# Query rows of an image scored in 3.5 tiles of 128, with the leftover rows gathered by DMAs from GpSimd

## The chip, the cores and the metric

The kernel runs on one core of one Trainium2 chip. The metric is the device time of one execution in microseconds. Three runs of the kernel before took 830.34 us in the median (828.73 to 830.89).

## What is computed

Four images, 12 heads, 448 rows, head size 64. The scores are mixed over the heads before the softmax and again after it; the result goes through an RMS norm and a gated MLP.

```
scores = scale * q @ k.T                          # (4, 12, 448, 448)
scores = einsum('bhij,hg->bgij', scores, w_pre)   # mix over heads, before
attn   = softmax(scores - max, axis=-1)           # sum + 1e-9 below
attn   = einsum('bhij,hg->bgij', attn, w_post)    # mix over heads, after
x      = (attn @ v) as (1792, 768)
xn     = x / rms(x) * rms_g
out    = (silu(xn @ w_gate) * (xn @ w_val)) @ w_out
```

## The kernel before

The attention is the first 347 us or so, the MLP the rest; the change is in the attention alone.

The rows of an image are cut into four chunks: three of 120 rows and one of 100, so that the score tiles hold 460 rows for 448. For each chunk n and each pair of heads hp, `qk_mm` (line 138) multiplies four times 64 query rows with the keys of one head (fp32, 64x64 weights, 448 columns) into two PSUM banks. `qk_evac` copies one bank to SBUF on VectorE (line 158, tile `st`) and one on ScalarE (line 160). A DMA then gathers from `st` (line 177) so that in the tile `r` the partitions are 12 heads of 5 rows. All 24 qk pairs of an image, six for each chunk, cost the same, whatever the chunk holds.

The loop `for t in range(T + 24)` in `part_a` has one step for each pair (n, p) of row groups, 92 in all: six in each of the first three chunks of an image and five in the last one, whose fifth step is half a step (one PSUM bank in place of two, for the last 10 rows). A step does:

- `premix` (line 186, PSUM tile `sp`): the mix over heads for 2 x 2 groups of 5 rows;
- `rowmax` on VectorE (line 193, `nm`), `expo` on ScalarE (line 200, `e`), both for two banks, then `norm`: line 207 (`t`) and 209 (`rp`) on VectorE, and line 212 (`wn`) on GpSimd, which scales the second mix by the reciprocal of the sums;
- `postmix` of the step before (line 227, tile `pm`), 28 small matmuls for a step, whose weights are `e` and whose input is `wn`; the half step issues the same 28, with two halves alike;
- one or two units of `av_mm` (line 271, tile `av`), the product with v of a pair of chunks finished earlier, 240 columns wide;
- the qk pair that `qk_at` sets for this step, for a chunk that is up to two chunks ahead. On TensorE its matmuls stand between those of premix: half of premix, half of qk, the other half of each;
- the copies of `pm` into `at_all` (line 240 on VectorE, 242 on ScalarE), and on GpSimd one operation of the sums of x (lines 294 to 309).

The order on every engine is the order in which the code issues it. `qk_at` holds one pair for each of the steps 0 to 84; the first eleven pairs are done ahead of the loop. All gathers in the loop go by the queue of SyncE; GpSimd issues none there.

Of the kernel before, what the change touches and what calls it, by code (L numbers as in the profile page):

```python
# [18 lines left out]
RH = 5  # L19
# [3 lines left out]
OFF = [0, 120, 240, 360]  # L23
# [26 lines left out]
def attention_moe(ctx: ExitStack, tc, q, k, v, wpre, wpost, mask, ident, wgv, wo, rms_g, out):  # L50
# [33 lines left out]
    wk_pre = cst.tile([128, 64], F32, name="wk_pre")  # L84
    wk = cst.tile([128, HR], F32, name="wk")

    msk = pro.tile([128, 2, RH], F32, name="msk", tag="ksm1")
    we = pro.tile([128, H], F32, name="we", tag="ksm2")
    wp = pro.tile([128, H], F32, name="wp", tag="ksm3")

    def load_consts():
        nc.sync.dma_start(msk.rearrange("p a r -> p (a r)"), mask)
        nc.sync.dma_start(we, wpre)
        nc.sync.dma_start(wp, wpost)

    def setup():
        nc.vector.tensor_scalar(we, we, D ** -0.5, None, ALU.mult)
        nc.vector.memset(wk_pre, 0.0)
        for i, (o, w) in enumerate(((wk_pre[:, :HR], we), (wk, wp))):
# [24 lines left out]
    held = []  # L124
# [7 lines left out]
    def qk_mm(n, hp):  # L132
# [7 lines left out]
        return [[lambda j=j, u=u: one(j, u) for u in range(2)] for j in range(2)]  # L140
# [8 lines left out]

    def qk_evac(n, hp, j):  # L150
        h, np_ = 2 * hp + j, PAIRS[n % NC]
        ps = qps[n, hp][j]
        if n == 0 and h < 1 or n == 1 and h < 2 * AHEAD:
            st = pro.tile([128, S], F32, name="st", tag="st", bufs=11)
        else:
            st = pq.tile([128, S], F32, name="st", tag="st", bufs=12)
        if j:
            nc.vector.tensor_copy(st, ps[:, :S])
        else:
            nc.scalar.activation(st, ps[:, :S], AF.Copy)  # L160
        for i, (lo, hi) in enumerate(((0, EARLY), (EARLY, 2 * np_)) if n == 0 else ((0, 2 * np_),)):
            w, at_ = RH * (hi - lo), 2 * RH * lo
            if h < H - 1:
                parts = [(h, 2 * RH, at_, 2 * w)]
            else:
                parts = [(h, RH, at_, w), (64, RH, at_ + w, w)]
            for row, k_, src, many in parts:
                dst = rt[n][row : row + (k_ - 1) * GAP + 1 : GAP, lo:hi]
                if i:
                    held.append((dst, st[src : src + many]))  # L170
                else:
                    turn = h if row < H else h + 1
                    if n:
                        eng = nc.gpsimd if n == 1 and 6 <= h < 2 * AHEAD else nc.sync
                    else:
                        eng = nc.sync if turn % 2 else nc.gpsimd if turn < 6 else nc.scalar
                    eng.dma_start(dst, st[src : src + many])

    def premix(n, p):
        ps = banks(ps_s, "sp", halves_of(n, p))  # L180
        sps[n, p] = ps

        def one(u, v_):
            sl = slice(64 * u, 64 * u + 64)
            o = ps[u][64 * v_ : 64 * v_ + 64, :S]
            nc.tensor.matmul(o, wk_pre[sl], rt[n][sl, 2 * p + v_], start=True, stop=True)  # L186

        return [[lambda u=u, v_=v_: one(u, v_) for v_ in range(2)] for u in range(len(ps))]
# [25 lines left out]
    def postmix(n, p):  # L214
        ps = banks(ps_m, "pm")
        e, w = et.pop((n, p)), wn.pop((n, p))
        for u in range(2):
            u_ = min(u, len(e) - 1)
            for c in range(JC):
                for m in range(2) if c < JC - 1 else (u,):  # L220
                    j = min(2 * c + m, S // JT - 1) * JT
                    for v_ in range(2):
                        sl = slice(64 * v_, 64 * v_ + HR)
                        at_ = u * (JC - 1) + c if c < JC - 1 else JB - 1
                        o = ps[v_][64 * m : 64 * m + JT, : JB * HR].rearrange("p (s a i) -> p s a i", s=2, a=JB)
                        w_ = w[sl, u_].rearrange("p (s i) -> p s i", s=2)
                        nc.tensor.matmul(o[:, :, at_], e[u_][sl, j : j + JT], w_, start=True, stop=True)  # L227
        pm[n, p] = ps

    def evac_a(n, p, v_):  # L230
# [4 lines left out]
        lo, hi = SLOTS[n]  # L235
        a = 2 * RH * p + RH * v_
        dst = at_all[:, lo : hi + 1 : hi - lo, :, a : a + RH]
        src = pm[n, p][v_][:, : JB * HR].rearrange("p (s x r) -> p s x r", s=2, r=RH)
        if v_:
            nc.vector.tensor_copy(dst, src)  # L240
        else:
            nc.scalar.activation(dst, src, AF.Copy)
# [5 lines left out]
    def width(k):  # L248
        return sum(4 * RH * PAIRS[n % NC] for n in BLOCKS[k])
# [23 lines left out]
    def av_copy(k, i):  # L273
        ns = BLOCKS[k]
        w, full = [2 * RH * PAIRS[n % NC] for n in ns], 2 * 2 * RH * PAIRS[ns[0] % NC]
        xt[k, i] = [p2[0].tile([128, 2, width(k)], F32, name=f"xt{k_}", tag=f"xt{k_}", bufs=3) for k_ in range(2)]
        for t, x in zip(xt[k, i], xps.pop((k, i))):
# [3 lines left out]
            else:  # L281
                nc.scalar.activation(t[:, :, :full], x[:, :, :full], AF.Copy)
                rest = x[:, :, full:].rearrange("p a (u i) -> p a u i", u=2)[:, :, :, : w[1]]
                nc.scalar.activation(t[:, :, full:].rearrange("p a (u i) -> p a u i", u=2), rest, AF.Copy)
# [100 lines left out]
    for i, a in enumerate([(n, hp) for n in range(1, NCHUNK) for hp in range(H // 2)][AHEAD:]):  # L385
        qk_at[i].append(a)
# [13 lines left out]
    for n in range(NCHUNK):  # L400
        b, c = divmod(n, NC)
        if n > 2:
            for i in range(2):
                job(6 * n - 16 + 3 * i, load_q, n, 3 * i, 3, nc.sync)
# [8 lines left out]
    for t, todo_ in enumerate(list(qk_at)):  # L413
        for n, hp in todo_:
            if n % NC == NC - 1 and n + 1 < NCHUNK:
                job(t + 1, load_k, n // NC + 1, hp)
# [22 lines left out]
    def part_a(extra):  # L439
# [30 lines left out]
        for t in range(T + 24):  # L470
# [46 lines left out]
            for a in qk_at[t][1:]:  # L517
                alone(qk_mm(*a))
                for j in range(2):
                    qk_evac(*a, j)  # L520
# [625 lines left out]
def layout(inputs):  # L1146
# [7 lines left out]
    qt = np.zeros((B, 2 * D, H // 2, SP_), np.float32)  # L1154
    qt[..., :S] = pairs(q)
    ql = np.zeros((B, 2 * D, NC, H // 2, 128), np.float32)
    for c, p in enumerate(PAIRS):
        u, r, t = np.meshgrid(np.arange(2), np.arange(RH), np.arange(2 * p), indexing="ij")
        i = np.minimum(OFF[c] + (u * 2 * p + t) * RH + r, SP_ - 1)
        ql[:, :, c, :, : 4 * RH * p] = qt[..., i.reshape(-1)]  # L1160
        if c == 0:
            i = np.concatenate([x.reshape(-1) for x in (i[..., :EARLY], i[..., EARLY:])])
            ql[0, :, c, :, : 4 * RH * p] = qt[0][..., i]
# [17 lines left out]
    mix = np.zeros((2, 64, H), np.float32)  # L1181
    row = np.zeros((2, 64, RH), np.float32)
    for u in range(2):
        for r in range(RH):
            at = GAP * r + (np.arange(H) + u) % H
            mix[u, at], row[u, at] = inputs["w_pre"], eye_r[r]
# [4 lines left out]
        "wpre": mix.reshape(128, H),  # L1191
        "wpost": halves(np.repeat(inputs["w_post"], RH, axis=0)),
        "mask": np.concatenate([row.reshape(128, RH), halves(np.tile(eye_r, (H, 1)))], axis=1),
# [23 lines left out]
```

## Time and profile before

| | us |
|---|---|
| median of three runs | 830.34 |
| the profiled execution | 833.58 |
| its span | 831.7 |
| TensorE busy | 799.6 (96%) |
| VectorE busy | 633.1 (76%) |
| ScalarE busy | 509.0 (61%) |
| GpSimd busy | 354.1 (43%) |

The profile is of one execution. Busy times are unions of instruction intervals. The ends of matmuls are modelled, so a TensorE shown as busy may be waiting inside a step. The granted clock of TensorE was full throughout (0.998 over the span). A step is told below by the time at which its first row maximum begins on VectorE.

### The profile page before, as it was taken

Reading aid. Unit: us, or ns where it says so; the run is one execution under the profiler, and the core shown is the slowest. Engines: PE = TensorE matmul, PEld = TensorE weight load, DVE = VectorE, ACT = ScalarE, POOL = GpSimd, SP = SyncE. Lnnn points to the kernel's source line nnn. Section 1 sums busy time; section 2 is a strip of 40 time slices with the busy share of each in tenths; the row PEclk is TensorE's granted clock in tenths of the full one; section 3 lists DMA queues with packets and bytes.
Section 4 is the critical chain, followed back from the end, with each engine's and each line's share of the span. In section 5 each row is a group of like instructions: output and inputs, shape, how many; then the busy total and the mean of one; then the engine's idle time right before and its main releaser. Section 6 shows DMA issues by size and latency. Waiting matters only on the chain.

```text
span 831.7 us, 27130 instructions
## 1 busy us (share of the span) xinstructions
PE 799.6 (96%) x10918; PEld 488.9 (59%) x10918; DVE 633.1 (76%) x1318; ACT 509.0 (61%) x1129; POOL 354.1 (43%) x467
## 2 busy tenths in 40 slices
PE   7899987999989999899999999999999999999998
PEld 2567766877767767655555555555555555555555
DVE  5777877797878877789589978997889776547562
ACT  3676767677767775774444554455445555969850
POOL 7212343353435435771533532525344358462310
PEclk9999999999999999999999999999999999999999
DMA  7778778667886665373446544753656345566641
GB/s 209 200 218 222 221 231 233 194 192 209 223 237 181 202 202 155 105 240 122 138 140 189 140 146 111 214 183 106 180 147 198 101 154 178 137 208 177 180 142 67
DMA packets 82383, 146.15 MB, mean 176 GB/s; under 512 B 10527, under 2 KB 73277, under 8 KB 82259
## 3 DMA queue, kind: packets, MB, share of 16 engines
q1 hardware_dynamic: 80462, 140.81, 56.5%
q0 software_dynamic: 832, 2.06, 1.0%
q8 instruction: 86, 1.41, 0.7%
q10 hardware_dynamic: 965, 1.56, 0.6%
q14 instruction: 38, 0.31, 0.1%
HBM read 72.83 MB, written 32.00 MB: 126 GB/s over the span
## 4 chain that ended last, share of the span: by engine, by line
PE 91%; issue 3%; DMA 3%; DVE 2%; ACT 1%; POOL 0%; ACTq 0%; SPq 0%; POOLq 0%; DVEq 0%
PE pm L227 9%; PE av L271 8%; PE qk L138 8%; PE sp L186 8%; PE pg L715 6%; PE pv L717 6%; PE pv L715 6%; PE pg L717 6%; PE pv L716 6%; PE pg L716 6%; PE po L717 6%; PE po L716 6%; PE po L715 6%; DMA r<-st 2%; DMA q<-in_q 1%
## 5 line engine op out<-in xcount | busy, mean ns | idle before, releaser
L200 ACT ACTIVATE e<-sp,nm 128x448 f32<-128x448 f32 x180 | 114.3, 638 | 90.8 <-DVE nm L193 88.7
L186 PE MATMUL sp<-r,wk_pre 64*64 64x448 f32 x720 | 163.9, 541 | 1.6 <-ACT e L200 1.0
L138 PE MATMUL qk<-k,q 64*64 64x448 f32 x768 | 153.6, 559 | 7.5 <-DMA q<-in_q 4.5
L193 DVE TENSOR_REDUCE nm<-sp 128x1 f32<-128x448 f32 x180 | 110.5, 620 | 42.1 <-PE sp L186 18.5
L212 POOL TENSOR_SCALAR wn<-wk,rp 128x60 f32<-128x60 f32 x180 | 60.8, 352 | 190.7 <-DVE rp L209 129.2
L227 PEld LDWEIGHTS pm<-wn,e 60*64 60x64 f32 x5152 | 110.3, 134 | 50.0 <-POOL wn L212 22.2
L227 PE MATMUL pm<-wn,e 60*64 60x60 f32 x5152 | 111.3, 220 | 15.2 <-issue 12.6
L763 POOL TENSOR_TENSOR sg<-sg,u 128x448 f32<-128x448 f32 x36 | 46.7, 1297 | 150.4 <-ACT sg L760 103.0
L271 PE MATMUL av<-at_all,v 64*64 64x240 f32 (+4 forms) x1728 | 95.9, 322 | 3.8 <-issue 3.7
L716 PE MATMUL pv<-x,wh 128*128 128x448 f16 x264 | 93.0, 352 | 0.0
L717 PE MATMUL pv<-x,wl 128*128 128x448 f16 x264 | 93.0, 352 | 0.0
L715 PE MATMUL pg<-x,wh 128*128 128x448 f16 x264 | 93.0, 352 | 0.0
L715 PE MATMUL pv<-x,wh 128*128 128x448 f16 x264 | 93.0, 352 | 0.0
L716 PE MATMUL pg<-x,wh 128*128 128x448 f16 x264 | 93.0, 352 | 0.0
L717 PE MATMUL pg<-x,wl 128*128 128x448 f16 x264 | 93.0, 352 | 0.0
L717 PE MATMUL po<-h,fac 128*128 128x448 f16 (+1 forms) x258 | 89.8, 348 | 0.0
L715 PE MATMUL po<-h,fac 128*128 128x448 f16 (+1 forms) x258 | 89.8, 348 | 0.0
L716 PE MATMUL po<-h,fac 128*128 128x448 f16 (+1 forms) x258 | 89.8, 348 | 0.0
L715 PEld LDWEIGHTS <-wh 128*128 128x128 f16 x528 | 51.7, 98 | 48.2 <-issue 0.2
L716 PEld LDWEIGHTS <-wh 128*128 128x128 f16 x528 | 51.7, 98 | 48.3 <-issue 0.3
L717 PEld LDWEIGHTS <-wl 128*128 128x128 f16 x528 | 51.7, 98 | 48.2
L271 PEld LDWEIGHTS av<-at_all,v 64*64 64x64 f32 x1728 | 71.3, 134 | 7.5 <-issue 6.8
(167 smaller groups left out, 1564.4 us busy)
## 6 DMA issues: line engine op xcount, KB each, us to landing
r<-st SPq DMA_DIRECT2D x117, 210.0 KB
hraw<-td SPq DMA_DIRECT2D x84, 224.0 KB
wraw<-in_wgv SPq DMA_DIRECT2D x20, 768.0 KB
td<-keep SPq DMA_DIRECT2D x48, 224.0 KB
wraw<-in_wo SPq DMA_DIRECT2D x12, 768.0 KB
r<-st SPq DMA_DIRECT2D x44, 175.0 KB
v<-in_v SPq DMA_DIRECT2D x24, 256.0 KB
k<-in_k SPq DMA_DIRECT2D x24, 224.0 KB
```

Of the source, the lines that this page charges most:

```text
L138: nc.tensor.matmul(ps[j][m, :S], qt[n][sl, hp, m], kt[n // NC, hp][sl], start=True, stop=True)
L186: nc.tensor.matmul(o, wk_pre[sl], rt[n][sl, 2 * p + v_], start=True, stop=True)
L193: nc.vector.tensor_reduce(t, ps[:, :S], AX.X, ALU.max, negate=True)
L200: nc.scalar.activation(e, ps[:, :S], AF.Exp, bias=nmx.pop((n, p, u)), accum_out=sm[n, p][:, u : u + 1])
L212: nc.gpsimd.tensor_scalar(wn[n, p][:, u], wk, r[:, u : u + 1], 1.0, ALU.mult, ALU.mult)
L227: nc.tensor.matmul(o[:, :, at_], e[u_][sl, j : j + JT], w_, start=True, stop=True)
L271: nc.tensor.matmul(x, vt[b, hp][sl, j, c_], a, start=(c_ == 0), stop=(c_ == JC - 1))
L715: nc.tensor.matmul(ps, a, xh[:, kk, at_], start=(kk == 0), stop=False)
L716: nc.tensor.matmul(ps, a, xl_[:, kk, at_], start=False, stop=False)
L717: nc.tensor.matmul(ps, a2, xh[:, kk, at_], start=False, stop=(kk == KT - 1))
L763: nc.gpsimd.tensor_tensor(h, sg, u, ALU.mult)
```

## The change

The first three chunks of an image now carry 8 more query rows each, from the end of the fourth, so that their qk tiles are full (128). The fourth chunk has 64 query rows and needs three qk steps in place of six: one step now takes four heads of 64 rows. The rows that don't fit into the groups of `r` go into a new tile `rest` (four slots), by small DMAs that GpSimd issues at the end of a step: two after each third qk pair of chunks 0 to 2, and four after the last one of chunk 3. Premix of the first and the last step of chunk 3 reads `rest` with weights of its own. An image has 450 rows in groups, the fourth chunk's last step stays a half one, and its postmix issues 14 matmuls. Chunks 2 and 3 are both 55 wide for the product with v (220 columns for the pair, 110 for the last chunks alone in place of 120). `st` becomes one tile with 12 slots.

```diff
-OFF = [0, 120, 240, 360]
+OFF = [0, 120, 240, 350]
+WIDE = [60, 60, 55, 50]
+TILES = [128, 128, 128, 64]
+SPLIT = 6
...
+        def two(j, i):
+            sl, u = slice(64 * j, 64 * j + 64), (i + j) % 2
+            nc.tensor.matmul(ps[i][64 * u : 64 * u + 64, :S], qt[n][sl, 2 * hp + i], kt[n // NC, 2 * hp + i][sl], start=True, stop=True)
+
+        f = one if n % NC < NC - 1 else two
+        return [[lambda j=j, u=u: f(j, u) for u in range(2)] for j in range(2)]
...
     def qk_evac(n, hp, j):
...
+        if n % NC == NC - 1:
+            for u in range(2):
+                gather(n, 2 * (2 * hp + j) + (u + j) % 2, st[64 * u : 64 * u + 64, at_], 0, SPLIT, False)
+            if hp == 2 and j:
+                for i in range(2):
+                    for u in range(2):
+                        later.append((rest[100 + 12 * u : 112 + 12 * u, slot(n - 3 + i)], st[64 * u + 60 + 2 * i : 64 * u + 62 + 2 * i, :6]))
         else:
...
+            if hp % 3 == 2 and j:
+                half = hp // 3
+                x = st[:, 6 * half : 6 * half + 6]
+                later.append((rest[30 * half : 30 * half + 30, slot(n)], x[120:125]))
+                later.append((rest[64 + 18 * half : 82 + 18 * half, slot(n)], x[125:]))
+
+    def rest_out():
+        for dst, src in later:
+            nc.gpsimd.dma_start(dst, src)
+        later.clear()
...
+        def rows(sl, i):
+            if not kind:
+                return rt[n][sl, i - 2 * last]
+            return rest[sl, slot(n - 3 + (i if p == 0 else 2))]
...
+        if len(e) == 1:
             for c in range(JC):
-                for m in range(2) if c < JC - 1 else (u,):
...
+                for m in range(2) if c < JC - 1 else (0,):
+                    for u in range(2):
+                        one(ps[u], u, u, c, m if c < JC - 1 else u, e[0], w[:, 0])
...
-        w = 2 * RH * PAIRS[ns[0] % NC]
+        w = WIDE[ns[0] % NC]
...
-    for i, a in enumerate([(n, hp) for n in range(1, NCHUNK) for hp in range(H // 2)][AHEAD:]):
-        qk_at[i].append(a)
+    starts, t_ = {}, -1
+    for n in range(1, NCHUNK):
+        for hp in range(H // 2 if n % NC < NC - 1 else H // 4):
+            if n == 1 and hp < AHEAD:
+                continue
+            t_ = max(t_ + (2 if n % NC == NC - 1 and hp == 2 else 1), first[n - 2] + 1 if n > 1 else 0)
+            starts.setdefault(n, t_)
+            qk_at[t_].append((n, hp))
...
         load_q(2, 3)
+        nc.gpsimd.memset(rest, 0.0)
+        rest_out()
         for hp in range(AHEAD):
             alone(qk_mm(1, hp))
             for j in range(2):
                 qk_evac(1, hp, j)
+        rest_out()
...
             if back(0) and t < T - 2:
                 norm(*back(0))
...
+            rest_out()
...
-    nc = bacc.Bacc("TRN2", target_bir_lowering=False, num_devices=1)
+    nc = bacc.Bacc("TRN2", target_bir_lowering=False, num_devices=1, dynamic_dma_scratch_size=8192)
```

What the table `qk_at` and the new DMAs do to the order is seen at three places. The first is TensorE in the second image, steps 33 to 35, before. `sp` is premix, `qk` the scores, `pm` the postmix of the step before, `av` the product with v; `k_0` to `k_5` are the keys of the six pairs of heads.

```order
L186 MATMUL sp<-r_123,wk_pre 64x448 x2
L138 MATMUL qk<-k_2_965,q_2207 64x448 x2
L186 MATMUL sp<-r_123,wk_pre 64x448 x2
L138 MATMUL qk<-k_2_965,q_2207 64x448 x2
L227 MATMUL pm<-wn,e 64x2x30 x28
L271 MATMUL av<-at_all,v_1_1173 64x240 x4
L271 MATMUL av<-at_all,v_1_1173 64x2x60 x4
L186 MATMUL sp<-r_123,wk_pre 64x448 x2
L138 MATMUL qk<-k_3_1036,q_2207 64x448 x2
L186 MATMUL sp<-r_123,wk_pre 64x448 x2
L138 MATMUL qk<-k_3_1036,q_2207 64x448 x2
L227 MATMUL pm<-wn,e 64x2x30 x28
```

The same place in the changed kernel:

```order
L226 MATMUL sp<-r_126,wk_pre 64x448 x4
L265 MATMUL pm<-wn,e 64x2x30 x28
L333 MATMUL av<-at_all,v_1_1124 64x220 x4
L333 MATMUL av<-at_all,v_1_1124 64x2x55 x4
L226 MATMUL sp<-r_126,wk_pre 64x448 x2
L149 MATMUL qk<-k_4_1012,q_2126 64x448
L149 MATMUL qk<-k_5_1014,q_2126 64x448
L226 MATMUL sp<-r_126,wk_pre 64x448 x2
L149 MATMUL qk<-k_4_1012,q_2126 64x448
L149 MATMUL qk<-k_5_1014,q_2126 64x448
L265 MATMUL pm<-wn,e 64x2x30 x28
```

Step 33 has no qk left and the product with v is narrower; step 34 has the third and last qk of chunk 7, with the keys of two pairs; step 35 has none again. Over the loop 73 steps have a qk pair in place of 85: it is gone from the steps 9, 11, 12, 33, 35, 56, 58, 79 and 81 to 84.

The second place is GpSimd at the steps 33 to 36, before. `wn` is the scaled second mix, `xt` and `sum` the sums of x.

```order
L212 TENSOR_SCALAR wn<-wk,rp 128x60 x2
L301 TENSOR_TENSOR xt_3029<-xt_3028 128x440
L212 TENSOR_SCALAR wn<-wk,rp 128x60 x2
L308 TENSOR_TENSOR xt_3029<-xt_3029 128x220
L212 TENSOR_SCALAR wn<-wk,rp 128x60 x2
```

And changed:

```order
L254 TENSOR_SCALAR wn<-wk,rp 128x60 x2
L364 TENSOR_TENSOR xt_2616<-xt_2615 128x420
L254 TENSOR_SCALAR wn<-wk,rp 128x60 x2
L210 DMA rest<-st 12x1x448 x4
L371 TENSOR_TENSOR xt_2616<-xt_2616 128x210
L254 TENSOR_SCALAR wn<-wk,rp 128x60 x2
```

Four DMA issues now stand between the `wn` of step 34 and that of step 35; after each third pair of a wide chunk two stand there.

The third place is TensorE at the half step of the first image, changed; before, every `pm` row there reads x28.

```order
L226 MATMUL sp<-rest,wk_pre 64x448
L145 MATMUL qk<-k_3_882,q_1208 64x448 x2
L226 MATMUL sp<-rest,wk_pre 64x448
L145 MATMUL qk<-k_3_882,q_1208 64x448 x2
L265 MATMUL pm<-wn,e 64x2x30 x28
L333 MATMUL av<-at_all,v_2_1282 64x240 x8
L226 MATMUL sp<-r_125,wk_pre 64x448 x2
L145 MATMUL qk<-k_4_1012,q_1208 64x448 x2
L226 MATMUL sp<-r_125,wk_pre 64x448 x2
L145 MATMUL qk<-k_4_1012,q_1208 64x448 x2
L265 MATMUL pm<-wn,e 64x2x30 x14
```

Premix of the half step reads `rest` on both halves of the partitions, and its postmix, one step later, has 14 matmuls.

## Rows read from the trace of the kernel before

**Rows 1.** The page: span, and busy time of each engine.

```profile
span 831.7 us, 27130 instructions
PE 799.6 (96%) x10918; PEld 488.9 (59%) x10918; DVE 633.1 (76%) x1318; ACT 509.0 (61%) x1129; POOL 354.1 (43%) x467
```

**Rows 2.** Windows: loop, five steps; us, then busy PE PEld DVE ACT POOL.

```profile
21.27:347.19 325.92, 303.74 (x7968) 230.32 (x7964) 254.47 (x673) 232.58 (x620) 133.37 (x293) 0.99 0.70 204
53.26:56.27 3.01, 3.01 (x74) 1.86 (x72) 2.41 (x7) 2.38 (x7) 0.60 (x2) 1.00 0.86 203
292.95:295.88 2.93, 2.93 (x92) 2.37 (x88) 2.52 (x6) 2.62 (x8) 1.00 (x3) 1.00 0.71 215
310.37:314.91 4.54, 3.87 (x108) 3.25 (x104) 3.03 (x10) 3.05 (x10) 1.41 (x5) 1.00 0.57 161
314.91:319.12 4.21, 4.03 (x109) 3.37 (x104) 2.62 (x6) 3.01 (x8) 2.61 (x5) 1.00 0.26 83
...
328.14:331.29 3.15, 3.15 (x108) 2.51 (x110) 2.40 (x10) 2.09 (x6) 1.87 (x8) 1.00 0.66 213
```

**Rows 3.** Timeline of one step, 292.7 to 295.9: start, length, engine, line.

```profile
292.73 0.60 POOL L212 TENSOR_SCALAR wn<-wk,rp 128x60 f32<-128x60 f32 x2 [1.38 <-DVE rp L209]
...
292.95 1.38 DVE L193 TENSOR_REDUCE nm<-sp 128x1 f32<-128x448 f32 x2 [0.39 <-PE qk L138]
...
293.10 1.19 PEld L227 LDWEIGHTS pm<-wn,e 60*64 60x64 f32 x54 [0.20 <-POOL wn L212]
...
294.27 0.83 PE L271 MATMUL av<-at_all,v 64*64 64x240 f32 x15
294.43 0.64 ACT L200 ACTIVATE e<-sp,nm 128x448 f32<-128x448 f32 x1
...
294.84 0.63 PE L186 MATMUL sp<-r,wk_pre 64*64 64x448 f32 x2
...
295.28 0.16 DVE L207 TENSOR_SCALAR t<-s 128x2 f32<-128x2 f32 x1
...
295.88 0.32 POOL L212 TENSOR_SCALAR wn<-wk,rp 128x60 f32<-128x60 f32 x1 [1.93 <-PE sp L186]
295.88 0.62 DVE L193 TENSOR_REDUCE nm<-sp 128x1 f32<-128x448 f32 x1 [0.17 <-PE sp L186]
```

**Rows 4.** Timeline, a step without qk: its two row maxima.

```profile
328.14 1.10 DVE L193 TENSOR_REDUCE nm<-sp 128x1 f32<-128x448 f32 x2
```

**Rows 5.** Groups by line, 21 to 347 us: busy, mean ns, idle before.

```profile
L186 PE MATMUL sp<-r,wk_pre 64*64 64x448 f32 x718 | 163.6, 541 | 1.5 <-ACT e L200 1.0 <-DMA r<-st 0.3
L138 PE MATMUL qk<-k,q 64*64 64x448 f32 x678 | 142.0, 547 | 1.7 <-issue 1.1 <-DMA q<-in_q 0.4 <-DVE t L207 0.2
...
L227 PE MATMUL pm<-wn,e 60*64 60x60 f32 x5064 | 109.7, 220 | 15.2 <-issue 12.6 <-DVE nm L193 1.1 <-POOL wn L212 0.7
...
L212 POOL TENSOR_SCALAR wn<-wk,rp 128x60 f32<-128x60 f32 x179 | 60.5, 352 | 190.0 <-DVE rp L209 128.5 <-PE sp L186 20.0 <-DVE square L602 7.6
...
L158 DVE COPY st<-qk 128x448 f32<-128x448 f32 x85 | 52.2, 614 | 0.0
...
L538 DVE TENSOR_SCALAR wac<-wac 128x384 f32<-128x384 f32 x8 | 2.7, 341 | 0.0
```

**Rows 6.** Timeline of GpSimd alone: the start, and two sums in the loop.

```profile
14.33 4.60 POOL L458 MEMSET r<- 128x5376 f32 x1
...
19.39 2.38 POOL L177 DMA_DIRECT2D r<-st  x4
23.93 0.61 POOL L212 TENSOR_SCALAR wn<-wk,rp 128x60 f32<-128x60 f32 x2 [2.15 <-DVE rp L209]
...
141.00 0.66 POOL L308 TENSOR_TENSOR xt<-xt 128x220 f32<-128x220 f32 x1
...
314.46 1.12 POOL L294 TENSOR_TENSOR xt<-xt,xt 128x440 f32<-128x440 f32 x1
```

**Rows 7.** The chain that ended last, 20 to 33 us: start, length, what.

```profile
26.84 3.55 DMA r<-st
```

More of the change, by code (lines that the diff above doesn't have):

```diff
@@ L148, in alone, with gather @@
         in_turn(*parts)
+    def gather(n, h, src, lo, hi, held_):
+        w, at_ = RH * (hi - lo), 2 * RH * lo
+        if h < H - 1:
+            parts = [(h, 2 * RH, at_, 2 * w)]
+        else:
+            parts = [(h, RH, at_, w), (64, RH, at_ + w, w)]
+        for row, k_, from_, many in parts:
+            dst = rt[n][row : row + (k_ - 1) * GAP + 1 : GAP, lo:hi]
+            x = src[from_ : from_ + many]
+            if held_:
+                held.append((dst, x))
+            else:
+                turn = h if row < H else h + 1
+                if n:
+                    eng = nc.gpsimd if n == 1 and 6 <= h < 2 * AHEAD else nc.sync
+                else:
+                    eng = nc.sync if turn % 2 else nc.gpsimd if turn < 6 else nc.scalar
+                eng.dma_start(dst, x)
@@ L161, in qk_evac @@
[L161 to L177, printed above, removed]
+        st = st_1 if n == 1 else st_all
@@ L181, in premix, with one @@
         sps[n, p] = ps
-        def one(u, v_):
+        last = n % NC == NC - 1
+        kind = int(last and p in (0, PAIRS[-1] - 1))
+        def rows(sl, i):
+            if not kind:
+                return rt[n][sl, i - 2 * last]
+            return rest[sl, slot(n - 3 + (i if p == 0 else 2))]
+        def one(u, v_, o):
             sl = slice(64 * u, 64 * u + 64)
-            o = ps[u][64 * v_ : 64 * v_ + 64, :S]
-            nc.tensor.matmul(o, wk_pre[sl], rt[n][sl, 2 * p + v_], start=True, stop=True)
-        return [[lambda u=u, v_=v_: one(u, v_) for v_ in range(2)] for u in range(len(ps))]
+            nc.tensor.matmul(o, wk_pre[sl, kind], rows(sl, 2 * p + v_), start=True, stop=True)
+        if len(ps) == 1:
+            return [[lambda u=u: one(u, 0, ps[0][64 * u : 64 * u + 64, :S])] for u in range(2)]
+        return [[lambda u=u, v_=v_: one(u, v_, ps[u][64 * v_ : 64 * v_ + 64, :S]) for v_ in range(2)] for u in range(2)]
     def rowmax(n, p):
@@ L1152, in pairs @@
         return x.reshape(B, H // 2, 2, S, D).transpose(0, 2, 4, 1, 3).reshape(B, 2 * D, H // 2, S)
[L1154 to L1163, printed above, removed]
+    qt = pairs(q)
+    ql = []
+    for b in range(B):
+        parts = []
+        for c in range(NC):
+            many = 2 * PAIRS[c] if c < NC - 1 else SPLIT
+            u, r, t = np.meshgrid(np.arange(2), np.arange(RH), np.arange(many), indexing="ij")
+            i = OFF[c] + WIDE[c] * u + RH * t + r
+            if c == 2:
+                i = np.where(t == 11, OFF[3] + WIDE[3] * u + 40 + r, i)
+            i = [i] if b or c else [i[..., :EARLY], i[..., EARLY:]]
+            i = [x.reshape(-1) for x in i]
+            at = np.arange(2 * RH)
+            if c < NC - 1:
+                more = [(30, 35, 45)[c] + (at // RH * WIDE[3] + at % RH)[:8]]
+            else:
+                more = [a + (at // RH * WIDE[3] + at % RH)[8:] for a in (30, 35)]
+            i = np.concatenate(i + [OFF[3] + x for x in more])
+            assert len(i) == TILES[c] and i.max() < S
+            parts.append(qt[b][..., i].reshape(2 * D, -1))
+        ql.append(np.concatenate(parts, axis=1))
+    ql = np.stack(ql)
     kl = pairs(k)
```

123 lines of the change are left out of this document (75 added, 48 removed).

## The prediction

> **What bounds the kernel now.** I read the head of the page first: TensorE is busy 96% of the span, the next engine 76% [rows 1]. That invites the reading that every microsecond taken off TensorE is a microsecond gained. The windows say where to doubt it. From the first step's row maximum to the 92nd's the loop takes 325.92 us [rows 2], 3.58 us a step, but an undisturbed step takes 2.93 us with qk and one unit of av, and 3.01 us with qk and no av at all [rows 2]. A whole unit of av (0.83 us, [rows 3]) costs such a step nothing, so TensorE's work is not what such a step lasts.
>
> So I followed one step through its timeline [rows 3]. The row maximum of step 77 starts at 292.95. The second exponential ends at 294.43 + 0.64 = 295.07, the sums are read at 295.28, and the scaled mix wn begins at 295.88: 2.93 us after the row maximum. The postmix of step 76 began to load at 293.10, 0.37 after its wn at 292.73. After it, postmix and av hold TensorE until premix of step 78 begins at 294.84, 1.74 later, and its row maximum starts 1.04 after that, at 295.88. These make a circle that closes every second step: postmix, av, premix, row maximum, exponential, sums, wn, postmix: 1.74 + 1.04 + 2.93 + 0.37 = 6.08 us for two steps, 3.04 for one, against 2.93 in this window. Neither the qk matmuls nor the copies of their result are links of that circle; qk only stands between the halves of premix and delays the second row maximum.
>
> Where a step has two units of av, TensorE does bind: steps 82 and 83 last 4.54 and 4.21 us with 3.87 and 4.03 of TensorE in them, and a step with two units and no qk lasts 3.15 [rows 2]. The rest of the average is single stalls, the first of them a gather that step 3 waits for from 26.84 on, 3.55 us [rows 7].
>
> **The change part by part.** All terms are against the profiled execution, 833.58 us, and carried over unchanged to the median of 830.34.
>
> Twelve steps lose their qk. *Steps 82 to 84* (two av): 4.54 and 4.21 become something like 3.15 with the same small stalls; I take the change in TensorE's busy time, 3.87 - 3.15 = 0.72 and 4.03 - 3.15 = 0.88, and 0.8 for the third: 2.4 gained. *Steps 9 and 12* (no av): VectorE's queue is the circle there, 2.41 busy of 3.01 [rows 2]; a copy of 0.614 [rows 5] goes out of it. I take 0.6 each: 1.2. Bounds for these: 0 and 0.8 each. *Steps 33, 56 and 79* (one av): two row maxima side by side take 1.10 [rows 4] where they take 1.38 around qk [rows 3], so the circle is 0.28 shorter. It could be nothing, since it helps only every second step's circle, or 0.61, a whole copy. I take 0.3, the row's: 0.9.
>
> *Steps 11, 35, 58 and 81* follow the four DMA issues on GpSimd. An issue in the start takes 2.38 / 4 = 0.595 us [rows 6], and the loop has none, so this is the one price without a row of its own place. From below, the issue is no cheaper than a wn of 0.352 [rows 5]; from above I allow twice the row, 1.2. At 0.595 four take 2.38. Wn of the step before starts about when this step's row maximum does (295.88 and 295.88, [rows 3]) and takes 0.6; then 2.38, then the sum at 0.66 [rows 6], so this step's wn starts 3.64 after the row maximum. Without qk it would be due 2.93 - 0.28 = 2.65 after it. It is late by 1.0, and against before by 0.7. Postmix is queued behind it on TensorE, and av and the next premix behind postmix. I charge 0.6 at 35, 58 and 81 (1.8 lost) and nothing at 11, where no sum stands between. Bounds: 0 (issue of 0.352) and 3.1 each (issue of 1.2).
>
> The pairs of issues: 21 fall in the loop. A pair, wn and the longest of the sums (1.12, [rows 6]) make 1.2 + 0.6 + 1.1 = 2.9 of a step of 2.93, so it just fits. GpSimd sits idle 190.0 us before the 179 wn, about 2.1 us for each step [rows 5]; that idle time is the cover. I charge 0.5 for all, between 0 and, at 1.2 for an issue, 21 x 0.6 = 12 less what the cover takes, some 6.
>
> [...]
>
> Narrower av: 36 units of the pairs of chunks 2 and 3 go from 240 to 220 columns. 0.83 x 20 / 240 = 0.07, less where half the matmuls are 120 wide: 0.06. A unit lies in every second circle, so half counts: 36 x 0.06 / 2 = 1.1; with 0.2 for the 110-wide units: 1.3 gained. Bounds 0 and 2.5.
>
> Postmix of the four half steps: 28 fewer records each at 109.7 / 5064 = 0.0217 us [rows 5], 0.6 of TensorE; half counts in the loop, all at the end: 1.0 gained together. Bounds 0 and 2.4.
>
> At the start GpSimd gets a memset of a third of one that took 4.60 (1.53), and six DMA issues at 0.595 ahead of the first wn: 5.1 us. It was through at 19.39 + 2.38 = 21.77, and wn started at 23.93 [rows 6], so this wn slips by 3.0. What follows it waits for the gather until 30.39 anyway [rows 7], so most is hidden; I charge 0.8, between 0 and 3. Copies into `st` wait for the new DMAs' reads of the slot; after chunks 7 and 11 the next write comes two steps later: 0.3 charged, up to 4.
>
> TensorE has 96 + 112 = 208 of its 7968 matmul records in the loop [rows 2] fewer, 2.6%. It stands 12.6 us before postmix waiting for nothing that the profile shows [rows 5]; in proportion that is 0.3, and with the same before other groups I take 0.4 gained. SyncE's queue keeps 52 gathers an image, the smaller ones in chunk 3. The MLP is untouched.
>
> Gained: 2.4 + 1.2 + 0.9 + 1.3 + 1.0 + 0.4 = 7.2. Lost: 1.8 + 0.5 + 0.8 + 0.3 = 3.4. Net 3.8: 833.6 becomes 829.8 in a profiled execution, and 830.3 becomes 826.5 in the median.
>
> **The rivals.**
>
> *TensorE binds after all.* Then all that it loses is gained: 96 qk records at 142.0 / 678 = 0.209 [rows 5] are 20.1, postmix 2.4, av 2.5: 25 us. For it speaks the 96% [rows 1] and that postmix and premix begin while others still run; against it the step without av. The three-microsecond circle would have to give way partly: at 60% it is 15 us, 815.
>
> *GpSimd becomes the bound, and the kernel is slower.* One mechanism: each DMA issue stands between two wn, and wn feeds postmix directly. It decides from an issue of about 0.75 us on, where a pair with its sum no longer fits into a step. At 0.9, a pair with wn and a sum between 0.66 and 1.12, say 0.85, takes 3.25 and costs 0.3 (21 of them 6.3); each of three fours makes wn late by 3.6 + 0.6 + 0.66 - 2.93 = 1.9 (5.7). That is 12.0 in place of 2.3: 9.7 more than in the sum, 836. For it: GpSimd's spans are rough, and wn has no slack. Against it: four issues in a row took 2.38.
>
> *Nothing comes of it.* The circle takes in what single steps gain, since the next step's circle was not shortened; only steps 82 to 84 and the end pay, 2.4 + 0.5, against 3.4 lost: 831, no change.
>
> **How the numbers follow.** The forecast has 0.50, TensorE as bound 0.20, no change 0.16, GpSimd 0.14. A measurement of this kernel tells 0.3% from no change, 2.5 us: faster means under 827.8. The forecast at 826.5, uncertain by 3, is faster in 0.70, the same in 0.26; the first rival always faster; the third faster in 0.25 and the same in 0.70; the second slower in 0.90. Together: faster 0.35 + 0.20 + 0.04 = 0.59, same 0.13 + 0.11 + 0.02 = 0.26, slower 0.15. The range goes from 813, past the first rival, to 835, almost at the second; its upper bound holds the issue costs up to 0.85 us.
>
> **What would show it.** In the profile after: qk in 672 records in place of 768 and busy about 20 us less; TensorE's busy time in the loop down by more than the loop itself; steps 82 to 84 near 3.2 us each; a step of one av without qk at 2.6 to 2.9; wn of steps 35, 58 and 81 waiting for nothing but GpSimd's own queue, with postmix idle before it; DMA issues near 0.6 us. I am wrong on the circle if single steps without qk get as short as 2.3 us, on GpSimd if issues in the loop take over 0.75 us, and on the start if the first wn comes more than 5 us after the 23.93 of before.

## The result and the profile after

The changed kernel takes 841.0 us (median of 8 runs, 834.2 to 866.2), the kernel before 831.0 beside it: a ratio of 1.0108, 95% interval 1.0062 to 1.0155. It is slower by 1.1%, not faster by 0.5%. Here and below a time is the median of all runs, while a ratio leaves out slow executions, those more than 1.5% above the fastest of their kernel, up to five of twelve. The profiled execution took 839.06 us, span 837.3. Of its engines, TensorE is busy as long as before, GpSimd 35 us longer [rows 1]:

```profile
span 837.3 us, 26834 instructions
PE 799.9 (96%) x10710; PEld 475.0 (57%) x10710; DVE 632.6 (76%) x1311; ACT 501.7 (60%) x1121; POOL 389.3 (46%) x532
```

The windows of the loop and of four of its steps (us, then busy PE, PEld, DVE, ACT and POOL, granted clock, DMA share, GB/s; their edges lie up to 0.06 us off the row maxima): the loop lasts 3.2 us longer than in [rows 2], although TensorE is busy 0.75 us less in it. Steps 9, 35 and 82 follow, and step 84:

```profile
22.12:351.31 329.19, 302.99 (x7792) 216.85 (x7788) 254.24 (x665) 225.32 (x611) 170.04 (x360) 0.99 0.70 195
59.29:61.93 2.64, 2.57 (x72) 1.37 (x72) 1.97 (x6) 2.24 (x6) 0.60 (x2) 1.00 0.67 211
147.45:150.10 2.65, 2.58 (x86) 1.97 (x88) 2.09 (x5) 2.45 (x10) 2.28 (x6) 1.00 0.65 167
315.75:320.47 4.72, 3.47 (x112) 2.85 (x114) 2.46 (x9) 2.52 (x8) 2.60 (x7) 1.00 0.41 114
323.46:329.11 5.65, 5.65 (x175) 4.86 (x176) 3.96 (x13) 2.30 (x7) 4.27 (x8) 1.00 0.04 14
```

The groups of the loop that answer to [rows 5]: qk is two groups now, 96 records fewer and 142.0 - 100.4 - 16.1 = 25.5 us less busy. The loads for postmix wait 44.6 us for wn (33.9 in one_row and 31.2 in no_rest, two experiments below), and the issues take 0.58 us each:

```profile
L265 PEld LDWEIGHTS pm<-wn,e 60*64 60x64 f32 x4980 | 102.8, 135 | 58.8 <-POOL wn L254 44.6 <-issue 10.3 <-DVE nm L235 0.5
L145 PE MATMUL qk<-k,q 64*64 64x448 f32 x486 | 100.4, 555 | 3.1 <-issue 2.6 <-DMA k<-in_k 0.5
L254 POOL TENSOR_SCALAR wn<-wk,rp 128x60 f32<-128x60 f32 x179 | 59.3, 344 | 151.1 <-DVE rp L251 99.2 <-PE sp L226 17.9 <-PE qk L145 7.5
L210 POOL DMA_DIRECT2D rest<-st x64 | 36.9, 580 | 5.2 <-issue 2.1 <-DMA rest<-st 1.5 <-ACT wac L820 0.4
L149 PE MATMUL qk<-k,q 64*64 64x448 f32 x96 | 16.1, 549 | 0.4 <-ACT st L191 0.4
```

GpSimd at the start (start, length, instruction, then the idle time before it): the first wn comes at 29.17, 5.2 us after the 23.93 of [rows 6].

```profile
20.43 1.61 POOL L530 MEMSET rest<- 128x1792 f32 x1
22.34 2.34 POOL L210 DMA_DIRECT2D rest<-st  x4 [0.30 <-POOL rest L530]
24.75 2.41 POOL L179 DMA_DIRECT2D r<-st  x4
27.16 0.56 POOL L210 DMA_DIRECT2D rest<-st  x1
28.48 0.56 POOL L210 DMA_DIRECT2D rest<-st  x1 [0.76 <-DMA rest<-st]
29.17 0.61 POOL L254 TENSOR_SCALAR wn<-wk,rp 128x60 f32<-128x60 f32 x2
```

The chain that ended last holds the transfers themselves (start, length, what): two leftover DMAs where [rows 7] has one gather, and in the loop a gather and a load of k behind each other, 14.9 us.

```profile
22.95 5.25 DMA rest<-st
28.48 6.40 DMA rest<-st
...
217.30 8.55 DMA r<-st
225.87 6.36 DMA k<-in_k
```

### The profile page after: what moved, and what is told of

Same layout as the page of the kernel before. It is cut to its first block, busy times and chain, and to the rows that moved or that the text cites. A ratio compares the mean times of both kernels' runs of the same rounds, so it can differ in the third digit from the quotient of the medians.

```text
span 837.3 us, 26834 instructions
## 1 busy us (share of the span) xinstructions
PE 799.9 (96%) x10710; PEld 475.0 (57%) x10710; DVE 632.6 (76%) x1311; ACT 501.7 (60%) x1121; POOL 389.3 (46%) x532
## 4 chain that ended last, share of the span: by engine, by line
PE 79%; DMA 7%; DVE 5%; issue 3%; POOL 3%; ACT 2%; SPq 1%; ACTq 0%; DVEq 0%; POOLq 0%
PE pm L265 7%; PE pg L785 6%; PE pv L786 6%; PE pg L787 6%; PE pv L785 6%; PE pg L786 6%; PE pv L787 6%; PE sp L226 6%; PE po L786 6%; PE po L785 6%; PE po L787 6%; PE av L333 6%; PE qk L145 5%; DMA r<-st 3%; DMA rest<-st 1%
## 5 line engine op out<-in xcount | busy, mean ns | idle before, releaser
L226 PE MATMUL sp<-r,wk_pre 64*64 64x448 f32 x672 | 149.9, 548 | 6.1 <-ACT e L242 3.0
L235 DVE TENSOR_REDUCE nm<-sp 128x1 f32<-128x448 f32 x180 | 108.8, 618 | 39.8 <-PE sp L226 27.5
L265 PEld LDWEIGHTS pm<-wn,e 60*64 60x64 f32 x5040 | 103.9, 135 | 59.2 <-POOL wn L254 45.0
L145 PE MATMUL qk<-k,q 64*64 64x448 f32 x576 | 113.0, 577 | 8.9 <-DMA q<-in_q 4.1
L333 PE MATMUL av<-at_all,v 64*64 64x240 f32 (+6 forms) x1728 | 91.7, 314 | 2.0 <-issue 1.9
L333 PEld LDWEIGHTS av<-at_all,v 64*64 64x64 f32 x1728 | 69.1, 133 | 4.7 <-issue 4.4
```

The source lines that it names most:

```text
L145: nc.tensor.matmul(ps[j][m, :S], qt[n][sl, hp, m], kt[n // NC, hp][sl], start=True, stop=True)
L226: nc.tensor.matmul(o, wk_pre[sl, kind], rows(sl, 2 * p + v_), start=True, stop=True)
L235: nc.vector.tensor_reduce(t, ps[:, :S], AX.X, ALU.max, negate=True)
L265: nc.tensor.matmul(o[:, :, at_], e_[sl, j : j + JT], w_[sl].rearrange("p (s i) -> p s i", s=2), start=True, stop=True)
L333: nc.tensor.matmul(x, vt[b, hp][sl, j, c_], a, start=(c_ == 0), stop=(c_ == JC - 1))
```

## The experiments

Ratios are against the kernel before on the same chip, five rounds each; "after" is the changed kernel at 1.0108 (1.0062 to 1.0155). Each edit is to it unless said. A difference between two ratios carries the intervals of both.

### What the 64 leftover DMAs cost, and whether GpSimd's issues are it

**no_rest**, the DMAs not issued:

```
-        for dst, src in later:
-            nc.gpsimd.dma_start(dst, src)
         later.clear()
```

> The changed kernel without the 64 DMAs into rest (the tile stays zero, so the leftover rows of every image are scored as zeros; all else is issued as in the changed kernel). Theory A, the DMAs on GpSimd cost all that is lost: the loop's start is no longer late (the changed kernel's row maximum of step 8 came 8.4 us late) and postmix no longer waits for a wn behind an issue; the time falls from 841 to 822 to 828 us, 3 to 9 below the kernel before. Theory B, the loss sits in the new layout itself (three qk steps with two pairs of heads, four gathers a step on SyncE, premix of rest): 835 to 841. Theory C, the start alone: the start's 8 us come back, the loop stays where it is: 832 to 834.

Measured: 824.4 us, 0.9897 (0.9857 to 0.9936). The rest of the change gains 1%, and the DMAs take away 2.1%.

**dmas_alone**, the kernel before with `st` as one tile, the tile `rest`, its memset and the same 64 DMAs, whose result nobody reads:

```
+        later.append((rest[30 * half : 30 * half + 30, slot(n)], x[120:125]))
+            rest_out()
```

> The kernel before with the tile rest, its memset and the same 64 DMAs added at the same places (nothing reads rest; st is one tile of 12 slots, the descriptor scratch 8192 as in the changed kernel). Theory A: 831 plus 12 to 18, so 843 to 849, more than the changed kernel, since nothing of the saving is there. Theory B: 831 to 835. Theory C: 838 to 840, with the first wn at 29 us and the loop of the kernel before behind it.

Measured: 856.0 us, 1.0275 (1.0242 to 1.0309), more than any theory gave: in the old schedule the same DMAs cost 2.7%. In its trace no copy and no matmul waits for them, only GpSimd's own issues (0.9 us).

**rest_sp**, SyncE issues them:

```
-            nc.gpsimd.dma_start(dst, src)
+            nc.sync.dma_start(dst, src)
```

> The changed kernel with the 64 DMAs issued by SyncE in place of GpSimd. Theory A: GpSimd is free, the first wn is at 25.5 us and postmix waits for wn as before: 829 to 835. If it is the landing of these DMAs, not their issue, that costs (copies into st wait for the slot to be read), the time stays at 838 to 842, as SyncE's queue was over 0.8 busy and lands them later still. Theory B: 841 or more.

Measured: 860.9 us, 1.0360 (1.0319 to 1.0402). With GpSimd free of them it is worse. They stand in SyncE's queue behind the gathers and hold the slots of `st`: copies into it wait 31.9 us on ScalarE and 27.5 on VectorE.

**start**, the memset of `rest` directly behind that of `r1`, chunk 1's DMAs left to step 0:

```
         nc.gpsimd.memset(r_all[1], 0.0)
+        nc.gpsimd.memset(rest, 0.0)
```

> The changed kernel with the start alone changed: the memset of rest directly behind that of the second r tile (GpSimd stood idle there until 7.2 us), and the rest DMAs of chunk 1 left to the first step of the loop, behind its wn. Theory A: the first wn comes at 24 to 25 us in place of 29.2, and 4 to 7 us come back: 834 to 837. Theory C, the start alone makes the loss: 831 to 834. If the late start was hidden behind the gather that step 3 waits for, as I predicted: 839 to 842.

Measured: 840.2 us, 1.0057 (1.0021 to 1.0093). At most a part of the loss.

**one_row**, the same issues, but one row each:

```
-        later.append((rest[30 * half : 30 * half + 30, slot(n)], x[120:125]))
+        later.append((rest[30 * half : 30 * half + 1, slot(n)], x[120:121, 5]))
```

> The changed kernel with its 64 leftover DMAs still issued by GpSimd at the same places, but each moving a single row of one head (1 x 448) in place of 12, 18 or 30 rows; so the rest tile gets only a 12th to a 30th of its rows. It keeps the issues and takes away the load and nearly all of the landing time. Known: the changed kernel 841.0 us, without the DMAs 824.4, before 831 to 833. Theory 1 (the 64 issues of 0.55 to 0.62 us stand ahead of the wn products in GpSimd's queue, and TensorE waits for wn): 838 to 842, nothing regained. Theory 2 (the copies into st wait until the slot's leftover DMAs, which land 3 to 9 us after the issue, have read it): 827 to 835. Theory 3 (the 3072 added packets hold up SyncE's gathers): 825 to 829.

Measured: 826.7 us, 0.9926 (0.9894 to 0.9958). The 64 issues cost 0.3% over no_rest, give or take 0.5%, of the 2.1%. So the wn that waits behind them is not the loss, and "issues ahead of wn" falls.

**other_src**, all rows, but read from the input k:

```
-        x = st[:, 6 * half : 6 * half + 6]
+        x = k[0]
```

> The changed kernel with the same 64 DMAs of the same shapes into the same rows of rest, but read from rows of the input k in DRAM, which nobody writes, in place of st; so the leftover scores are not the right ones. Issues and traffic stay, the copies into st wait for no leftover DMA any more, and the issue waits for no copy. Theory 1 (issues ahead of wn): 838 to 842. Theory 2 (st held until the DMAs have read it): 826 to 832. Theory 3 (packets): 838 to 842.

Measured: 832.2 us, 0.9988 (0.9948 to 1.0029). Against one_row the bytes cost about 0.6%, give or take 0.5%; the last 1.2% goes when `st` isn't read. The packets change with it (3584 and 1792 bytes in place of 5376). What is dear, the hold on the slots, the reading or the packets, was open.

### The hold on the slots

**alt**, the halves of `st` in strict turn, so that a half is written again three steps after its DMAs:

```
+        turn = n // NC % 2 if n > 1 else 0
+        my = (at_ + 6 * turn) % H
```

> The changed kernel with the two halves of st taken in strict turn: the short chunk uses one half and the chunk after it begins with the other, so that a half is written again three heads' pairs (some 8 to 9 us) after its leftover DMAs were issued, in place of one step (2.6 us) at the ends of the images. Nothing else changes. Theory 1 (issues ahead of wn): 839 to 841, nothing. Theory 2 (st held): the waits for the slot in steps 36, 59 and 82 (sums 2.74, 1.82 and 1.16 us late there) go, 832 to 836. Theory 3 (packets): 839 to 841.

**spread**, at most one or two issues a step (at three image ends the last ones then read slots that the next chunk has already written):

```
-            rest_out()
+            rest_out(2 if len(later) > 2 else 1)
```

> The changed kernel with at most one leftover DMA issued in a step, or two where more than two are waiting, in place of two or four behind each other; the same 64 DMAs, some of them one to three steps later. Theory 1 (issues ahead of wn): the late wn of steps 35, 58 and 81 (1.15 to 1.70 us after t in place of 0.44) and those beside sum operations shrink, 830 to 836. Theory 2 (st held): the DMAs start later and the slots come free later, 840 to 846. Theory 3 (packets): 838 to 841.

**rows**, the slots interleaved, to cut the packets:

```
+        my = at_ % 6 * 2 + at_ // 6
```

> The changed kernel with the twelve slots of st interleaved: heads 0 to 5 of a chunk take the even slots, heads 6 to 11 the odd ones. Nothing else changes, but the six rows that a leftover DMA reads in one partition no longer lie behind each other, so it can't put three of them into one packet of 5376 bytes. Known: in the changed kernel 368 such packets between 45 and 350 us took 705 ns each, where three packets of 1792 bytes at 93 ns take 279; read from DRAM the same rows went in packets of 3584 and 1792 bytes at 198 and 107 ns, and the kernel took 832.2 in place of 841.0. Theory 2a (slots held, and held long because the long packets from 2 to 5 partitions are slow): packets of 1792 bytes, landing near 4.5 us in place of 5.8, 829 to 835. Theory 2b (slots held, and reading from so few partitions is slow however the packets are cut): 838 to 842. Theory 3 (the load alone): 839 to 841.

Measured: alt 838.8 us, 1.0057 (1.0018 to 1.0097); spread 851.4, 1.0230 (1.0176 to 1.0284); rows 841.4, 1.0116 (1.0082 to 1.0150). Spread shows that a hold can cost: VectorE's copies wait 17.2 us for leftover DMAs there. Alt takes the waits of copies away and gains half a percent, and its interval overlaps that of after. The edit of rows missed its aim: the packets were still of 5376 bytes, at 639 ns in the mean, so it tells nothing of their cutting; it stands as a second measurement of after.

**many_parts**, as many rows, each from a partition of its own, from the slot that is written again last; **wide_hold**, the same from the slot that is written again first; **few_free**, the old partitions, but the last slot read six times:

```
-  x[120:125]
+  x[:30, 5]                                   (many_parts)
+  x[:30, 0]                                   (wide_hold)
+  x[120:125, 5:6].to_broadcast([5, 6, S])     (few_free)
```

> The changed kernel with the same 64 DMAs of 12, 18 and 30 rows into the same places of rest, but each read from one slot of st, a row from each of as many partitions, in place of six slots of 2 to 5 partitions; so the leftover scores are not the right ones. The bytes stay, the packets can't be longer than 1792 bytes, one slot in six is held and that one the last to be written again. Theory 2a and 2b (slots held until slow transfers have read them): 826 to 833, packets near 95 ns. Theory 3 (the load alone): 836 to 841.

> As the run with one row from each of 12, 18 or 30 partitions (833.2, ratio 0.9983; packets of 3584 and 1792 bytes at 256 and 93 ns), but read from the first slot of each half (0, or 6) in place of the last: the slot that the next chunk writes first, so it is held as in the changed kernel. The leftover scores are not the right ones. Theory H (the hold of a slot until its leftover DMAs have landed makes the 1.2% between that run and the changed kernel): 838 to 842, with copies into st waiting for leftover DMAs. Theory P (the slow packets of 5376 bytes from 2 to 5 partitions make it, through the other transfers on the same 16 engines): 831 to 835, as packets stay short.

> The changed kernel with the same 64 DMAs from the same 2, 3 or 5 partitions, but the last slot of the half read six times in place of six slots; so the leftover scores are not the right ones. The slot that is held is the last that the next chunk writes. Theory H (hold): 831 to 835, no copy into st waits for them. Theory P (slow packets from few partitions): packets of 5376 bytes at 550 to 700 ns as in the changed kernel, 836 to 842.

Measured: many_parts 833.2 us, 0.9983 (0.9945 to 1.0021); wide_hold 831.1, 0.9964 (0.9926 to 1.0002); few_free 838.8, 1.0081 (1.0045 to 1.0118). In many_parts the packets were of 3584 and 1792 bytes (257 and 93 ns in the mean), longer than expected. In few_free no copy waits for a leftover DMA, and it loses 0.8%, nearly all: the slow reading needs no hold. The trace of wide_hold, of an execution of 843.3 us, shows no waiting copy either, since its DMAs land in 4.6 us (median) in place of 5.8; so it is a hold that never made anyone wait. Theory P stands. Theory H falls by few_free, and by far_few below, where copies do wait.

### Why the reading is slow

**far_few** and **step_four**, the same shapes from partitions far apart, and from partitions four apart:

```
-  x[120:125]      x[125:]
+  x[0:125:31]     x[10:103:46]    (far_few)
+  x[0:17:4]       x[84:93:4]      (step_four)
```

> The changed kernel with the same 64 DMAs in number and shape (2, 3 or 5 partitions by six slots of st), but the partitions far apart: 0, 31, 62, 93 and 124; 10, 56 and 102; 0 and 96 or 16 and 112, in place of 120 to 124, 125 to 127 and two neighbours; so the leftover scores are not the right ones. The slots are held as in the changed kernel. Theory P1 (slow because neighbouring partitions are read at once): packets of 5376 bytes near 3 x 93 = 280 to 400 ns, 831 to 836. Theory P2 (slow because few partitions are read, wherever they lie): 600 to 720 ns, 838 to 842.

> The changed kernel with the same 64 DMAs in number and shape, read from partitions four apart: 0, 4, 8, 12 and 16; 84, 88 and 92; two that are four apart for the short chunk. So the leftover scores are not the right ones. Known: from neighbours packets took 705 ns (1.0108), from partitions 31 to 96 apart 385 ns (1.0014). Theory D (what counts is the distance): four apart lies near neighbours, 550 to 700 ns, 836 to 842. [...]

Measured: far_few 835.9 us, 1.0014 (0.9983 to 1.0045); step_four 835.2, 1.0008 (0.9974 to 1.0043). The packets of 5376 bytes took 386 and 367 ns in the mean in place of 705. Four apart is as good as far, so theory D, the distance, falls. These two are the clean comparison with after and few_free: the packets are the same in number and size.

GpSimd's DMA queue between 45 and 350 us shows it: packets, MB, and the share that its packets took of the time of 16 engines. After:

```profile
q0 software_dynamic: 2595, 2.00, 5.7%
```

one_row:

```profile
q0 software_dynamic: 1728, 0.10, 0.4%
```

many_parts:

```profile
q0 software_dynamic: 1728, 1.98, 3.0%
```

few_free:

```profile
q0 software_dynamic: 2592, 2.00, 5.6%
```

far_few:

```profile
q0 software_dynamic: 2592, 2.00, 3.3%
```

step_four:

```profile
q0 software_dynamic: 2592, 2.00, 3.2%
```

The same 2 MB take 5.6 to 5.7% from neighbours and 3.0 to 3.3% from elsewhere, and the kernels fall into the same two groups, 1.008 to 1.012 and 0.996 to 1.001. The number of packets does not sort them: few_free, far_few and step_four have the same. The groups are less clean than these numbers: start and the versions that read the neighbours with other changes besides (alt above, three more below) have slow packets too and lie between, at 1.004 to 1.006.

The gathers on SyncE's queue are late with the slow packets. SyncE issues about 177 gathers in this stretch. Of them 8 to 13 took more than 1 us in no_rest, one_row, many_parts, far_few and step_four; in after it was 23, in few_free 21, their sum 154.3 and 153.8 us in place of 138.9 to 143.8. At the start the last eight gathers of chunk 0 and the six of chunk 1 take SyncE 20.2 us after and 20.3 in few_free, 18.5 in step_four, 16.8 in far_few and 14.6 in no_rest. After:

```profile
17.39 6.82 SPq L526 DMA_DIRECT2D r<-st  x8
24.32 13.34 SPq L179 DMA_DIRECT2D r<-st  x6
```

no_rest:

```profile
17.99 7.03 SPq L524 DMA_DIRECT2D r<-st  x8
25.14 7.56 SPq L179 DMA_DIRECT2D r<-st  x6
```

The traces also show where in the execution this counts. The row maximum of step 8 in after, few_free, far_few and step_four:

```profile
55.53 0.60 DVE L235 TENSOR_REDUCE nm<-sp 128x1 f32<-128x448 f32 x1
55.72 0.60 DVE L235 TENSOR_REDUCE nm<-sp 128x1 f32<-128x448 f32 x1
51.10 0.60 DVE L235 TENSOR_REDUCE nm<-sp 128x1 f32<-128x448 f32 x1
50.32 0.60 DVE L235 TENSOR_REDUCE nm<-sp 128x1 f32<-128x448 f32 x1
```

And from there to the row maximum of the last step, in the same order (window, us, then busy times as above):

```profile
55.53:351.25 295.72, 277.34 (x7272) 202.02 (x7276) 234.46 (x618) 207.25 (x565) 156.56 (x330) 1.00 0.70 197
55.72:351.93 296.21, 275.94 (x7272) 205.37 (x7276) 232.38 (x619) 207.57 (x565) 156.41 (x330) 0.99 0.69 197
51.10:348.50 297.40, 276.52 (x7272) 201.52 (x7276) 233.05 (x619) 207.40 (x565) 156.55 (x330) 1.00 0.67 197
50.32:349.73 299.41, 277.53 (x7272) 203.20 (x7276) 233.33 (x618) 207.58 (x565) 156.56 (x330) 1.00 0.67 196
```

Reading neighbours makes step 8 late by 4.4 to 5.4 us. Behind step 8 it makes nothing longer that these traces show, although there, too, 22 gathers in after take over 1 us on SyncE, and 10 and 13 in far_few and step_four. What does differ behind step 8 are the kernels without packets of 5376 bytes: 287.1 us in one_row, 290.0 in many_parts, 290.7 in other_src and no_rest, where those that have them take 291.9 (rows_alt_early, below) to 299.6 (alt); left aside are spread, whose copies wait, and wide_hold, whose traced execution took 843.3 us against a median of 831.1. Whether their shorter or fewer packets do that, no run separates. Each of these is one execution, and executions of one kernel lie several us apart; so this places the loss and does not size it.

That waits of copies are not the price is seen once more in far_few. Who waited for `rest` there (us, times), and how long its DMAs took to land:

```profile
L210 POOL DMA_DIRECT2D rest<-st x64: 547/566/622, 22.1 to 312.3; - x64
...
  DVE st L189: 6.6, 3
  ACT st L191: 4.3, 2
...
DMA to landing us min/median/max: 2.6/4.5/8.9
```

And after:

```profile
L210 POOL DMA_DIRECT2D rest<-st x64: 547/568/622, 22.3 to 315.0; - x64
...
  DVE st L189: 5.7, 3
  ACT st L191: 3.3, 3
...
DMA to landing us min/median/max: 3.0/5.8/8.8
```

The copies wait longer in far_few, which is the faster; what differs is the landing.

Why the packets are slow from neighbouring partitions (705 ns) and not from partitions four apart (367 ns), no run shows.

### Versions that keep the result

**alt_early**, alt with chunk 0's DMAs ahead of the load of q and the memset of `r2`; **rows_alt_early**, that with the slots interleaved; **one_each**, alt_early with one issue a step; **one_each_act**, that from ScalarE's queue:

```
+        rest_out()
         load_q(2, 0)
         nc.gpsimd.memset(r_all[2], 0.0)
```

```
+            rest_out(1 if t else 4)                                 (one_each)
+                (nc.gpsimd if many == 4 else nc.scalar).dma_start   (one_each_act)
```

> The halves of st in strict turn, as in the run of that alone (838.8, ratio 1.0057), and the start put in another order on GpSimd: the memset of rest directly behind that of r1, the four leftover DMAs of chunk 0 ahead of the load of q and the memset of r2 (so some 6 to 8 us earlier), those of chunk 1 left to step 0. All in the same packets. At the start the copies of chunk 2 into st wait for these four DMAs to land. Theory 2 (slots held): most of the 8.4 us that row max of step 8 was late at (55.5 in place of 47.1) goes, 829 to 834. Theory 1 (issues ahead of wn) or 3 (load): 837 to 840, as the issues and the bytes stay.

> All three together: slots of st interleaved, halves in strict turn, chunk 0's leftover DMAs early. Without any leftover DMA it was 824.4. Theory 2a: 824 to 830, faster than the kernel before (831) by 0.2 to 0.8%. Theory 2b: 828 to 834. Theory 3: 834 to 840.

> The version with the halves of st in turn and the early start (834.2, ratio 1.0056), with one leftover DMA issued in a step in place of two or four; with the halves in turn each still reads its slots before they are written again. Theory H: 832 to 836, nothing left to win, or the later ones hold a little more. Theory P: fewer slow packets at a time, 828 to 833.

> The same with ScalarE's queue issuing the leftover DMAs of steps 1 and later (one in a step); GpSimd keeps the eight of the start. When SyncE issued them the packets were of 1792 bytes at the usual 93 ns. An issue on ScalarE took 0.78 us at the start, and ScalarE idles some 0.6 to 1.9 us a step before its exponentials: 56 issues of 0.78 us are 44 us, of which 0 to 20 show. Theory P: packets short, 824 to 829 and the part of the issues that shows, so 826 to 838. Theory H: 834 and that part, 834 to 846.

Measured: alt_early 834.2 us, 1.0056 (1.0022 to 1.0090); rows_alt_early 835.8, 1.0039 (1.0010 to 1.0068); one_each 837.6, 1.0039 (1.0003 to 1.0076); one_each_act 916.9, 1.1033 (1.0983 to 1.1082). The first three gain 0.5 to 0.7% on after, with intervals that overlap its own, and none beats the kernel before: the slow packets are all still there (in alt_early at 717 ns, GpSimd's queue at 5.9% of the time of 16 engines). ScalarE's queue is far worse than either theory said, though an issue took 0.74 us where 0.78 was expected. Its packets were of 1792 bytes, at 173 ns in the mean:

```profile
L213 ACTq DMA_DIRECT2D rest<-st x56: 630/744/822, 35.4 to 402.2; - x56
```

56 of these are 42 us and the loss is 84, so more than the issues is late; what, stays open.

A version with its leftover rows in partitions four or more apart, and its right result, was not tried. By step_four (1.0008) and far_few (1.0014) that alone would come level with the kernel before and not beat it. It would cost, too, as the author reads the code, though no run shows it: with rows taken out between, the other 120 rows of a chunk no longer lie behind each other, and each of SyncE's gathers would have to be split.

## Why the prediction was wrong

- **The gains were right in sum, in part by luck.** 7.2 us were forecast; no_rest shows 1.03% of 830.3, 8.6 us (5.3 to 11.9). But the terms that can be followed step by step, from the trace before to that of no_rest, came out smaller than charged: steps 9 and 12 gave 0.8 of 1.2, steps 33, 56 and 79 gave 0.4 of 0.9, steps 82 to 84 gave 1.8 of 2.4. Step 83 fell to 3.12, as asked, but step 82 to 4.10 and not to 3.2, and step 84, which has 5.65 us of TensorE's work in 5.65 us after, had taken 5.90. Where the rest was gained was not followed.
- **TensorE as the bound falls; the circle was not refuted, nor was it shown.** That rival asks for 25 us, and no_rest, with all of TensorE's savings and none of the DMAs, gains 8.6. The sign named for the circle, TensorE's busy time down by more than the loop, decides nothing: after, the loop grew (302.99 us busy in 329.19), and in no_rest TensorE's busy time fell by 6.4 us (to 297.39) and the loop by 9.2 (to 316.77).
- **The issues were right.** 0.58 us each in the loop where 0.595 was taken, and wn of step 35 came when forecast. GpSimd around it, in the columns of the start:

```profile
147.33 0.60 POOL L254 TENSOR_SCALAR wn<-wk,rp 128x60 f32<-128x60 f32 x2 [1.39 <-DVE rp L251]
148.30 2.27 POOL L210 DMA_DIRECT2D rest<-st  x4 [0.37 <-ACT wac L820]
150.55 0.60 POOL L371 TENSOR_TENSOR xt<-xt 128x210 f32<-128x210 f32 x1
151.08 0.63 POOL L254 TENSOR_SCALAR wn<-wk,rp 128x60 f32<-128x60 f32 x2
```

  It starts 3.60 us after the row maximum at 147.48, forecast 3.64. That it is so close is chance: 0.37 us of waiting for ScalarE, which the sum lacks, make up for shorter parts. The rival with GpSimd as bound gave nearly the right time (836) by the wrong mechanism: one_row keeps every issue and is faster than before.
- **The failing step is the price of the DMAs behind their issue.** The sum holds 64 issues and no term for the 2 MB that they carry in the loop. "Copies into `st` wait for the new DMAs' reads of the slot [...] 0.3 charged, up to 4" was the only place where a transfer of the new DMAs had a price, and it was put on the wrong thing. The runs show about 0.4 to 0.6% (3 to 5 us) for the bytes (one_row against many_parts, wide_hold and other_src, each give or take 0.5%) and 0.7 to 1.1% (6 to 9 us) for reading them from neighbouring partitions (far_few and step_four against few_free, after and rows).
- **The start is where that error was largest.** It was charged 0.8 us, with bounds of 0 and 3, because "What follows it waits for the gather until 30.39 anyway". The gathers themselves came later. The first wn came 5.2 us late, past the mark at which the prediction called itself wrong there, and the row maximum of step 8 started at 55.5 us after, at 47.1 before: 8.4 us. The issues are not the reason: one_row, which has them all, is there at 47.2 and no_rest at 48.0; with the bytes from elsewhere it is 49.8 (many_parts) to 51.1 (far_few). The neighbours' 4.4 to 5.4 us at step 8 are part of the 6 to 9 us above; where the rest of these falls stays open. Start, which changed only the order there, was at 52.9.

## What to carry to other kernels

A leftover DMA had three prices here: the issue on its queue (0.58 us each in the loop), the landing for whoever waits (5.8 us in the median after), and the load on the 16 engines (5.7% of their time between 45 and 350 us), which went with late issues on another queue (23 of SyncE's 180 gathers over 1 us, 8 of 174 in no_rest). Price all three, at the start of a kernel above all: here step 8 came 8.4 us late after, and 0.1 late in one_row. A packet that reads a few neighbouring partitions took nearly twice as long as one of the same bytes from partitions spread out (705 ns after, 386 in far_few and 367 in step_four), and no row of the issuing engine showed it (an issue took 568 ns in the median after, 566 in far_few and 564 in step_four). To find which price counts, issue it with one row, then with all rows from elsewhere.

## What the runs showed of the hardware that was not expected

- A packet of 5376 bytes read by GpSimd's DMAs took 705 ns in the mean from neighbouring partitions (120 to 127 in most; after) and 367 ns from partitions four apart (step_four).
- It shows on another queue: SyncE's gathers, at a median of 0.76 to 0.77 us an issue, go over 1 us about twice as often or more (23 of 180 after, 10 and 13 of 177 in far_few and step_four, 8 of 174 in no_rest). At the start that goes with a step 8 that is 4.4 to 5.4 us late; behind it, with no longer loop.
- The same DMAs issued by ScalarE, one a step, made the kernel 10% slower (one_each_act, 916.9 us, 1.1033).
